# Queries' product of linear attention in float32 on four 64 by 64 tiles of TensorE, in one step with the keys' product

## The chip, the cores and the metric

One core of a Trainium2 chip runs the whole program. The metric is the device time of one execution in microseconds (us), the median of several runs. Engines are TensorE (PE, matmuls; PEld, its weight loads), VectorE (DVE), ScalarE (ACT), GpSimd (POOL) and SyncE (SP), whose queue issues all the loads and stores named here.

## What is computed

Linear attention with 8 batches, 8 heads, 576 positions and 64 columns a head, then two MLPs on the 4608 tokens (512 wide, 2048 inside):

```python
q_s = exp(q - max(q, -1));  q_s = q_s / (sum(q_s, -1) + 1e-09)     # over a head's 64 columns
k_s = exp(k - max(k, 2));   k_s = k_s / (sum(k_s, 2) + 1e-09)      # over the 576 positions
kv  = einsum('bhsd,bhse->bhde', k_s, v)                            # 64 x 64 a head
x   = einsum('bhsd,bhde->bhse', q_s, kv)                           # as rows of 512
h = x @ w_in;  x = (h - tanh(h)) @ w_out                           # first MLP
h = x @ w_in2; g = P(h) / (Q(h) + 1e-6);  out = g @ w_out2         # second MLP, P cubic, Q quadratic
```

## The kernel before

The tokens are cut into 9 blocks of 512. Block 0's attention is computed in front of everything (the loop of 8 stages `s`). After it come 144 steps n: step n does the first product of slice f = n % 16 of block j = n // 16 of the first MLP (`first_product`, 12 matmuls into `hps`), then the second product of the step two before it (12 matmuls into `acc`). The attention of block j is worked off during the 16 steps of block j - 1, by the table `work`, which holds for each step the pieces of attention and loads that are issued in it. Blocks 1 to 8 have 4 pairs p of heads each (two heads of 64 columns fill the 128 partitions). In a step the table's single functions go out first (`front`), then the first product, the second product, and then (`turn`) the matmuls of attention; their readers follow at the step's end (`follow`). The second MLP comes after step 143.

Matmuls of the MLPs run on float32r operands that are split in a high and a low part (`mm3`, lines 79 to 82: high x high, high x low, low x high). The queries' product does the same: `q_parts` (block 0) and `q_split` (later) split the queries with a copy on ScalarE and a subtraction on VectorE, `kv_parts` splits the keys' product into `bd` with two copies on ScalarE and two small operations on VectorE (lines 516 and 520), and `q_mm` runs `mm3` with `bd` as a 128 x 128 block diagonal matrix. A block of 512 tokens touches one or two batches (`spans`), with a `bd` of each, so there are three or six matmuls a pair. `q_out` copies the result to `xr` on ScalarE (line 658). The keys' product `kv_mm` (line 500) is float32: 5 groups of positions x 2 heads, each head writing its half of the partitions, 65 columns (the last is the sum).

From block 2 on the keys' maximum over positions goes through DRAM (`kv_max`, `kv_squares`, `kv_fetch`, `kv_join`, then `kv_sub`, `kv_exp`), and the queries are transposed through DRAM (`q_squares`, `q_fetch`). Pool `ps_a` has two accumulators (banks), which these products share. In the table the keys' product of pair p of block j stands in step 16(j - 1) + 3p + 4 and the queries' product one step later (block 1: 3p + 3 and 3p + 5).

In block 0 of the MLP, ScalarE, VectorE and GpSimd also decode the weights from the 64-bit numbers in which they arrive (`decode`, lines 131 to 158). Later they prepare parts of weights and of the second MLP's input (`errands`, `x2_units`).

Of the kernel before, what the change touches and what calls it, by code (L numbers as in the profile page):

```python
# [18 lines left out]
P = 128  # L19
# [24 lines left out]
def attention_moe_moe2_kernel(ctx, tc, q, k, v, w1, w2, w3, w4, ca, cb, out):  # L44
# [348 lines left out]
    bd = {}  # L393
    for par in range(2):
        for p in range(NPAIR):
            bd[par, p] = tuple(
                bdp.tile([P, P], F32R, tag=f"bd{par}{p}{part}", name=f"bd{par}{p}{part}") for part in "hl"
            )
# [3 lines left out]
    FIRST = {"qr": 4, "ke": 4, "qe": 4, "mx": 2, "mc": 2, "qm": 4, "qs": 4, "rs": 4, "qh": 2, "ql": 2}  # L402
# [91 lines left out]
    def kv_mm(b, p):  # L494
        e, vs = kv_state.pop((b, p)), vt.pop((b, p))
        pool, tag = (ps_h, "h") if b == 0 and p >= 2 else (ps_a, "a")
        ps = pool.tile([P, NB], F32, tag=tag, name="kvps")
        for g in range(G):
            for h in range(2):
                PE.matmul(  # L500
                    ps[h * D:(h + 1) * D, 0:D + 1], e[:, g, h, :], vs[:, h, g, :], start=g == 0, stop=g == G - 1
                )
        kv_state[b, p] = ps

    def kv_sum(b, p):
        rs = att_tile(b, [P, 1], F32, "rs")
        DVE.tensor_scalar_add(rs, kv_state[b, p][:, D:D + 1], EPS_S)
        DVE.reciprocal(rs, rs)
        kv_state[b, p] = kv_state[b, p], rs

    def kv_parts(b, p):
        ps, rs = kv_state.pop((b, p))
        hi, lo = bd[b % 2, p]
        heads = [(slice(h * D, (h + 1) * D), slice(0, D)) for h in range(2)]
        for r, c in heads:
            ACT.activation(out=hi[r, r], in_=ps[r, c], func=AF.Copy, scale=rs[r])

        def low():
            for r, c in heads:
                DVE.scalar_tensor_tensor(  # L520
                    out=lo[r, r], in0=ps[r, c], scalar=rs[r], in1=f32(hi[r, r]), op0=ALU.mult, op1=ALU.subtract
                )

        return low

    def kv_norm(b, p):
        kv_sum(b, p)
        return kv_parts(b, p)
# [84 lines left out]
    def q_parts(j, p):  # L613
        ps = q_state[j, p]
        qh = att_tile(j, [P, NB], F32R, "qh")
        ql = att_tile(j, [P, NB], F32R, "ql")
        ACT.copy(out=qh, in_=ps)
        DVE.tensor_tensor(out=ql, in0=ps, in1=f32(qh), op=ALU.subtract)
        q_state[j, p] = (qh, ql)


# [9 lines left out]
    def q_fetch(j, p):  # L631
        d = q_state[j, p].rearrange("(q i) (g b t) -> b i g q t", i=SQ, g=4, t=SQ)
        t = att_tile(j, [P, NB], F32R, "ql")
        for b in range(P // SQ):
            SP.dma_start(out=f32(t)[b * SQ:(b + 1) * SQ].rearrange("i (g q t) -> i g q t", g=4, t=SQ), in_=d[b])
        q_state[j, p] = t

    def q_split(j, p):
        t = q_state[j, p]
        qh = att_tile(j, [P, NB], F32R, "qh")  # L640
        ACT.copy(out=qh, in_=f32(t))  # L641
        DVE.tensor_tensor(out=t, in0=f32(t), in1=f32(qh), op=ALU.subtract)  # L642
        q_state[j, p] = (qh, t)

    def q_mm(j, p):
        qh, ql = q_state[j, p]
        ps = (ps_a if j else ps_acc).tile([P, NB], F32, tag="a" if j else f"acc{p}", name="xps")
        for b, p0, p1 in spans(j):
            def cols(a):
                return a if p1 - p0 == P else a.rearrange("x (g p) -> x g p", g=4)[:, :, p0:p1]  # L650
# [12 lines left out]
    Q = (q_max, q_sub, q_exp, q_sum, (q_turn, q_parts), (q_mm, q_out))  # L663
    Q_LATER = (q_max, q_sub, q_exp, q_sum, q_squares, q_fetch, q_split, (q_mm, q_out))
# [6 lines left out]
    def turn(todo):  # L671

        got = []
        for fn, args in todo:
            if isinstance(fn, tuple):
                fn[0](*args)
# [9 lines left out]
    work = {s: [] for s in range(NBLK * KF)}  # L686
    for j in range(1, NBLK):
        for p in range(NPAIR):
            at = (j - 1) * KF + 3 * p
            if j < B:  # L690
                for fn, s in zip(KV, (0, 1, 2, 3, 3)) if j == 1 else zip(KV_LATER, (-2, -2, 2, 3, 3, 4, 4)):
                    work[max(at + s, 0)].append((fn, (j, p)))
            for fn, s in zip(Q, (-1, 0, 1, 2, 4, 5)) if j == 1 else zip(Q_LATER, (-3, -2, -1, 0, 1, 3, 4, 5)):
                work[max(at + s, 0)].append((fn, (j, p)))
        for p in range(2, NPAIR + 2):
            at = (j - 1) * KF + 3 * p
            to, tp = j + p // NPAIR, p % NPAIR
            if to < B:
                work[at - 3].append((load_k, (to, tp)))
                work[at - (2 if to == 1 else 1)].append((load_v, (to, tp)))  # L700
            if to < NBLK:
                work[at - (4 if to == 1 else 6)].append((load_q, (to, tp)))

    with tc.manual_schedule():

        make_identity(nc, identity)
        for tiles in bd.values():
            for t in tiles:
                DVE.memset(f32(t), 0.0)
# [16 lines left out]
        for s in range(NPAIR + 4):  # L726
# [13 lines left out]
            at(3, kv_sum, q_parts)  # L740
            for low in at(3, kv_parts):
                low()
# [293 lines left out]
```

## Time and profile before

| | us |
|---|---|
| median of 3 runs | 1672.69 (1672.29 to 1672.77) |
| the profiled execution | 1671.62 |
| its span, first to last instruction | 1669.8 |
| TensorE busy | 1626.7 |
| VectorE busy | 1166.4 |
| ScalarE busy | 1022.2 |
| GpSimd busy | 1038.9 |
| attention in front | 0 to about 45 |
| steps 0 to 143 | about 38 to 895 |

A row of the timeline gives an instruction's start and length; the length of a matmul holds its way through the array, so rates are read from starts. Float32r operands stand as f32 there, and `128*64` is rows by columns of the part of the array that is used. A float32 matmul stands as two records.

### The profile page before, as it was taken

What the parts mean: (1) busy time and instruction counts of PE and PEld (TensorE: products, weight loads), DVE (VectorE), ACT (ScalarE), POOL (GpSimd) and SP (SyncE); (2) the same over time, 40 slices, a digit from 0 to 9 for tenths busy, and PEclk for the clock granted to TensorE, in tenths of its full rate; (3) what the DMA queues carried; (4) which work ended last, traced back from release to release, by engine and by line L of the source; (5) the groups of instructions that cost most, each with busy time, mean ns of one, the idle gap of its engine ahead of it and who ended that gap; (6) DMA issues with size and microseconds to landing.
All of it is one profiled execution on the core that took longest, in us unless ns stands there. A gap on an engine that the chain in (4) does not pass through costs nothing.

```text
span 1669.8 us, 26578 instructions
## 1 busy us (share of the span) xinstructions
PE 1626.7 (97%) x9096; PEld 1392.8 (83%) x9096; DVE 1166.4 (70%) x1948; ACT 1022.2 (61%) x1825; POOL 1038.9 (62%) x875
## 2 busy tenths in 40 slices
PE   5899999999999999999999999999999999999998
PEld 3677788888888888888887999999989899999996
DVE  8987666676765666653213777787878787878787
ACT  5675444554454544453325777777777777777775
POOL 4222737365463727364343888888888777777776
PEclk8999999999999999999999999999999999999999
DMA  8553665757474765633198576767676767666640
GB/s 225 166 171 94 185 180 153 208 155 215 128 221 116 206 172 150 201 121 107 52 318 306 181 268 212 274 219 269 223 263 228 243 216 248 216 247 216 209 148 26
DMA packets 250728, 323.73 MB, mean 194 GB/s; under 512 B 119009, under 2 KB 185569, under 8 KB 241377
## 3 DMA queue, kind: packets, MB, share of 16 engines
q1 hardware_dynamic: 250592, 322.03, 60.0%
q8 instruction: 72, 1.18, 0.3%
q14 instruction: 64, 0.52, 0.1%
HBM read 249.04 MB, written 72.93 MB: 193 GB/s over the span
## 4 chain that ended last, share of the span: by engine, by line
PE 88%; DVE 5%; ACT 3%; DMA 2%; issue 1%; SPq 1%; POOL 0%; DVEq 0%; ACTq 0%; POOLq 0%
PE acc L80 15%; PE acc L81 15%; PE acc L82 14%; PE z L830 12%; PE y L830 9%; PE hps L80 7%; PE hps L82 7%; PE hps L81 7%; DMA u<-x2d 1%; PE kvps L500 1%; ACT m L133 1%; DVE m L147 1%; ACT e L131 0%; DVE m L134 0%; PE xps L81 0%
## 5 line engine op out<-in xcount | busy, mean ns | idle before, releaser
L340 POOL TENSOR_TENSOR gl<-t,gh 128x512 fp32r<-128x512 f32 x128 | 175.2, 1369 | 322.7 <-ACT gh L336 295.0
L336 ACT CAST gh<-t 128x512 fp32r<-128x512 f32 x128 | 79.7, 622 | 273.2 <-PE acc L82 156.3
L887 POOL TENSOR_TENSOR n<-n,r 128x512 f32<-128x512 f32 x144 | 186.1, 1293 | 96.2 <-ACT r L884 90.8
L887 POOL TENSOR_TENSOR n<-n,n 128x512 f32<-128x512 f32 x144 | 186.5, 1295 | 36.5 <-ACT n L871 36.5
L945 DVE TENSOR_TENSOR t<-hps,t 128x512 f32<-128x512 f32 x128 | 87.5, 684 | 158.8 <-ACT t L942 158.4
L887 POOL TENSOR_TENSOR n<-n,h 128x512 f32<-128x512 f32 x144 | 187.2, 1300 | 9.7 <-DMA xl<-x2d 9.6
L942 ACT ACTIVATE t<-hps 128x512 f32<-128x512 f32 x144 | 85.9, 597 | 115.5 <-PE hps L82 92.7
L841 ACT COPY sums<-z 128x256 f32<-128x256 f32 x144 | 53.6, 372 | 134.2 <-PE z L830 134.2
L867 ACT ACTIVATE n<-h,coef 128x512 f32<-128x512 f32 x144 | 116.5, 809 | 0.3 <-POOL n L887 0.3
L897 DVE CAST gh<-a 128x512 fp32r<-128x512 f32 x144 | 99.6, 692 | 16.1 <-DVE a L893 0.5
L900 DVE TENSOR_TENSOR gl<-a,gh 128x512 fp32r<-128x512 f32 x144 | 99.6, 692 | 15.2 <-DVE gh L897 0.5
L893 DVE SCALAR_TENSOR_TENSOR a<-a,n 128x512 f32<-128x512 f32 x144 | 100.0, 694 | 14.1 <-POOL n L887 8.2
L876 DVE SCALAR_TENSOR_TENSOR a<-h,absb,a 128x512 f32<-128x512 f32 x144 | 107.5, 746 | 3.0 <-ACT a L861 2.9
L861 ACT ACTIVATE a<-h,coef 128x512 f32<-128x512 f32 x144 | 100.5, 698 | 3.4 <-DVE gl L900 3.4
L890 DVE SCALAR_TENSOR_TENSOR a<-a,r 128x512 f32<-128x512 f32 x144 | 99.3, 690 | 0.8 <-ACT r L884 0.8
L879 ACT ACTIVATE r<-a,bias_q 128x512 f32<-128x512 f32 x144 | 97.0, 674 | 0.0
L884 ACT ACTIVATE r<-r 128x512 f32<-128x512 f32 x144 | 91.1, 633 | 4.6
L864 ACT ACTIVATE h<-h 128x512 f32<-128x512 f32 x144 | 89.1, 619 | 1.0 <-DVE h L852 0.8
L848 DVE TENSOR_TENSOR h<-y,sums 128x256 f32<-128x256 f32 x72 | 30.5, 424 | 57.8 <-PE y L830 57.7
L852 DVE TENSOR_TENSOR h<-y,top 128x512 f32<-128x512 f32 x72 | 49.7, 690 | 26.2 <-ACT top L841 25.8
L604 POOL TENSOR_TENSOR qe<-qe,qs 128x512 f32<-128x512 f32 x36 | 39.2, 1088 | 46.0 <-DVE qs L603 46.0
L642 DVE TENSOR_TENSOR ql<-ql,qh 128x512 fp32r<-128x512 f32 x28 | 26.9, 960 | 50.6 <-ACT qh L641 48.7
(366 smaller groups left out, 5272.6 us busy)
## 6 DMA issues: line engine op xcount, KB each, us to landing
u<-x2d SPq DMA_DIRECT2D x78, 256.0 KB, 5.3
raw<-in_moe_w_in_dram SPq DMA_DIRECT2D x32, 512.0 KB, 4.2
raw<-in_moe_w_out_dram SPq DMA_DIRECT2D x32, 512.0 KB, 4.2
x2d<-raw SPq DMA_DIRECT2D x64, 256.0 KB, 3.2
x2d<-xr SPq DMA_DIRECT2D x56, 256.0 KB, 3.1
wa0h<-wa0d SPq DMA_DIRECT2D x9, 1024.0 KB, 5.2
wa1h<-wa2d SPq DMA_DIRECT2D x9, 1024.0 KB, 5.1
wa2h<-wa4d SPq DMA_DIRECT2D x9, 1024.0 KB, 5.0
```

The costliest lines, as they stand in the source:

```text
L80: PE.matmul(o, lhi, rhi, start=start, stop=False)
L81: PE.matmul(o, lhi, rlo, start=False, stop=False)
L82: PE.matmul(o, llo, rhi, start=False, stop=stop)
L340: eng.tensor_tensor(out=gl, in0=g, in1=f32(gh), op=ALU.subtract)
L830: PE.matmul(o, w, x[:, xc], start=m in (1, 5) and c == k == 0, stop=c == 1 and k == 2, skip_group_check=True,)
L861: ACT.activation(out=new(t, "a", ps_a), in_=t["h"], func=AF.Abs, scale=b0)
L867: ACT.activation(out=new(t, "n1"), in_=t["h"], func=AF.Identity, scale=a3, bias=a2)
L876: DVE.scalar_tensor_tensor(out=t["a"], in0=t["h2"], scalar=b1, in1=t["a"], op0=ALU.mult, op1=ALU.add)
L887: return lambda t: POOL.tensor_tensor(out=t[a], in0=t[a], in1=t[b], op=op)
L893: DVE.scalar_tensor_tensor(out=t["a"], in0=t["a"], scalar=2.0, in1=t["n0"], op0=ALU.subtract, op1=ALU.mult)
L897: DVE.tensor_copy(out=t["g"][0], in_=t["a"])
L900: DVE.tensor_tensor(out=t["g"][1], in0=t["a"], in1=f32(t["g"][0]), op=ALU.subtract)
```

## The change

The queries are kept in float32 and not split: `q_copy` takes the place of `q_parts` in block 0, and `q_split` goes away, as the fetch lands in the tile that the matmul reads. `bd` holds the normalized keys' product in float32, the two heads side by side in columns (128 x 2 x 64), without a low part. For blocks 1 to 8 `q_mm` runs four float32 matmuls a span, each with 64 rows and 64 columns of the array: head h reads its 64 partitions and writes bank `ps[h]`, half `to` of the 512 columns goes to partitions 0 to 63 or 64 to 127. It takes two accumulators of `ps_a` and hands the first to `kv_mm`, which writes its result beside the queries' result, in columns 256 to 320. For block 0 `q_mm` runs two float32 matmuls of 128 rows by 64 columns. `q_out` copies four pieces of 64 x 256 instead of one of 128 x 512. The table is written anew: the queries' products stand in steps 4, 8, 11 and 14 of the 16 (block 1: 6, 9, 12 and 14), the keys' product of pair p > 0 in the step of the queries' product of pair p - 1, that of pair 0 two steps before the block's first (block 2: in its first); maxima, transposes, fetches and loads go by these steps.

```diff
-                bdp.tile([P, P], F32R, tag=f"bd{par}{p}{part}", name=f"bd{par}{p}{part}") for part in "hl"
+        (par, p): bdp.tile([P, 2, D], F32, tag=f"bd{par}{p}", name=f"bd{par}{p}")
...
-    def kv_mm(b, p):
+    def kv_mm(b, p, room=None):
...
-        ps = pool.tile([P, NB], F32, tag=tag, name="kvps")
+        ps = pool.tile([P, NB], F32, tag=tag, name="kvps") if room is None else room
...
-                    ps[h * D:(h + 1) * D, 0:D + 1], e[:, g, h, :], vs[:, h, g, :], start=g == 0, stop=g == G - 1
+                    ps[HEADS[h], HALF:HALF + D + 1], e[:, g, h, :], vs[:, h, g, :], start=g == 0, stop=g == G - 1
...
-            ACT.activation(out=hi[r, r], in_=ps[r, c], func=AF.Copy, scale=rs[r])
-        def low():
-                DVE.scalar_tensor_tensor(
-                    out=lo[r, r], in0=ps[r, c], scalar=rs[r], in1=f32(hi[r, r]), op0=ALU.mult, op1=ALU.subtract
+            ACT.activation(out=bd[b % 2, p][r, h], in_=ps[r, HALF:HALF + D], func=AF.Copy, scale=rs[r])
...
-    def q_parts(j, p):
-        ACT.copy(out=qh, in_=ps)
-        DVE.tensor_tensor(out=ql, in0=ps, in1=f32(qh), op=ALU.subtract)
+    def q_copy(j, p):
+        t = att_tile(j, [P, NB], F32, "qh")
+        ACT.copy(out=t, in_=q_state[j, p])
...
-    def q_split(j, p):
-        ACT.copy(out=qh, in_=f32(t))
-        DVE.tensor_tensor(out=t, in0=f32(t), in1=f32(qh), op=ALU.subtract)
...
-            mm3(cols(ps), *bd[b % 2, p], cols(qh), cols(ql), True, True)
+        if j == 0:
+            for h, r in enumerate(HEADS):
+                PE.matmul(ps[r], bd[0, p][:, h], t, start=True, stop=True)
+        ps = [ps_a.tile([P, NB], F32, tag="a", name="xps") for _ in range(2)]
+        for b, p0, p1 in sorted(spans(j), key=lambda x: x[2] - x[1]):
+            for to in range(2):
+                for h, r in enumerate(HEADS):
+                    PE.matmul(
+                        cols(ps[h][HEADS[to], 0:HALF]), bd[b % 2, p][r, h], cols(t[r, to * HALF:(to + 1) * HALF]),
+                        start=True, stop=True,
+                    )
+        return ps[0]
...
-            ACT.copy(out=xr[:, p, :], in_=ps)
+            for to in range(2):
+                for h, r in enumerate(HEADS):
+                    ACT.copy(out=xr[r, p, to * HALF:(to + 1) * HALF], in_=ps[h][HEADS[to], 0:HALF])
...
+    kv_at = {(1, p): 3 * p + 3 for p in range(NPAIR)}
+    q_at = {(1, p): (6, 9, 12, 14)[p] for p in range(NPAIR)}
+            q_at[j, p] = first(j) + (4, 8, 11, 14)[p]
+                kv_at[j, p] = q_at[j, p - 1] if p else first(j) - (2 if j > 2 else 0)
+    q_from = {(j, p): 3 * p if j == 1 else at - 7 for (j, p), at in q_at.items()}
-                for fn, s in zip(KV, (0, 1, 2, 3, 3)) if j == 1 else zip(KV_LATER, (-2, -2, 2, 3, 3, 4, 4)):
+                for fn, s in zip(KV, (-3, -2, -1, 0, 0)) if j == 1 else zip(KV_LATER, (-4, -4, -2, -1, -1, 0, 0)):
...
-        for tiles in bd.values():
-            for t in tiles:
-                DVE.memset(f32(t), 0.0)
+        for p in range(NPAIR):
+            for h, r in enumerate(HEADS):
+                DVE.memset(bd[0, p][r, 1 - h], 0.0)
```

## Rows read from the trace of the kernel before

**Rows 1.** The page: busy time of each engine; shares of the chain that ended last.
```profile
PE 1626.7 (97%) x9096; PEld 1392.8 (83%) x9096; DVE 1166.4 (70%) x1948; ACT 1022.2 (61%) x1825; POOL 1038.9 (62%) x875
PE 88%; DVE 5%; ACT 3%; DMA 2%; issue 1%; SPq 1%; POOL 0%; DVEq 0%; ACTq 0%; POOLq 0%
```
**Rows 2.** Windows: stretch, busy us (and instructions) by engine, clock, DMA share, GB/s.
```profile
25.00:50.00 25.00, 16.64 (x81) 12.48 (x80) 22.29 (x48) 19.10 (x38) 8.98 (x7) 0.78 0.60 172
125.00:150.00 25.00, 23.31 (x122) 18.50 (x121) 22.42 (x43) 17.83 (x34) 3.77 (x3) 1.00 0.40 114
175.00:200.00 25.00, 23.61 (x139) 19.17 (x138) 17.64 (x27) 11.24 (x22) 19.32 (x16) 1.00 0.66 194
425.00:450.00 25.00, 25.00 (x115) 20.81 (x114) 17.19 (x30) 12.15 (x23) 8.46 (x7) 1.00 0.39 117
```
**Rows 3.** Timeline of TensorE around a keys' product: start us, length us, instruction.
```profile
365.98 0.39 PE L82 MATMUL acc<-gh,wb0l 128*128 128x512 f32 x1
366.30 0.80 PE L500 MATMUL kvps<-vt,ke 128*64 128x65 f32 x20
367.03 0.50 PE L80 MATMUL hps<-xh,wa1h 128*128 128x512 f32 x1
367.37 0.39 PE L81 MATMUL hps<-xl,wa1h 128*128 128x512 f32 x1
...
367.83 0.40 PE L80 MATMUL hps<-xh,wa1h 128*128 128x512 f32 x1
```
**Rows 4.** Timeline around queries' products of blocks 4, 7 and 8: matmul before, second after.
```profile
372.39 0.40 PE L82 MATMUL acc<-gh,wb0l 128*128 128x512 f32 x1
373.57 0.40 PE L81 MATMUL hps<-xl,wa1h 128*128 128x512 f32 x1
...
709.72 0.40 PE L82 MATMUL acc<-gh,wb3l 128*128 128x512 f32 x1
711.13 0.39 PE L81 MATMUL hps<-xl,wa3h 128*128 128x512 f32 x1
...
748.78 0.40 PE L82 MATMUL acc<-gh,wb0l 128*128 128x512 f32 x1
749.94 0.40 PE L81 MATMUL hps<-xl,wa1h 128*128 128x512 f32 x1
```
**Rows 5.** Timeline of block 0: four float32 transposes of 128 columns, and one alone.
```profile
70.42 0.60 PE L610 MATMUL qps<-identity,qe 128*128 128x128 f32 x4
56.20 0.27 PE L476 MATMUL kvps<-identity,mc 128*128 128x128 f32 x1
```
**Rows 6.** Keys' product's group, 45 to 150 us: busy, mean ns | idle, releaser.
```profile
L500 PE MATMUL kvps<-vt,ke 128*64 128x65 f32 x80 | 3.2, 226 | 4.5 <-ACT ke L492 4.3
```
**Rows 7.** Chain pieces of the front; groups of 45 to 150 us; ScalarE's 256-column copy.
```profile
18.80 0.03 DVE ql L618
...
19.41 0.27 DVE bd00l L520
...
L618 DVE TENSOR_TENSOR ql<-qps,qh 128x512 fp32r<-128x512 f32 x4 | 2.8, 691 | 1.1 <-ACT qh L617 1.1
L520 DVE SCALAR_TENSOR_TENSOR bd11l<-kvps,rs,bd11h 64x64 fp32r<-64x64 f32 x2 | 0.6, 284 | 0.8 <-ACT bd11h L516 0.8
L658 ACT COPY xr<-xps 128x512 f32<-128x512 f32 x4 | 2.4, 593 | 0.0
L841 ACT COPY sums<-z 128x256 f32<-128x256 f32 x144 | 53.6, 372 | 134.2 <-PE z L830 134.2
```
**Rows 8.** Chain pieces behind block 0, and TensorE's waits from 155 to 900 us.
```profile
163.27 4.33 DMA ke<-kd
167.62 1.12 DVE mx L550
168.77 1.77 DVE ke L482
...
PE kvps L500 <- ACT ke L492: 1.4, 2, 1.2
```

More of the change, by code (lines that the diff above doesn't have):

```diff
@@ L391, in attention_moe_moe2_kernel @@
     absb = const.tile([P, 2], F32, name="absb")
[L393 to L396, printed above, removed]
-                bdp.tile([P, P], F32R, tag=f"bd{par}{p}{part}", name=f"bd{par}{p}{part}") for part in "hl"
-            )
+    bd = {
+        (par, p): bdp.tile([P, 2, D], F32, tag=f"bd{par}{p}", name=f"bd{par}{p}")
+        for par in range(2) for p in range(NPAIR)
+    }
+    HEADS = slice(0, D), slice(D, P)
     G = -(-S // P)
     REST = S - (G - 1) * P
-    FIRST = {"qr": 4, "ke": 4, "qe": 4, "mx": 2, "mc": 2, "qm": 4, "qs": 4, "rs": 4, "qh": 2, "ql": 2}
+    FIRST = {"qr": 4, "ke": 4, "qe": 4, "mx": 2, "mc": 2, "qm": 4, "qs": 4, "rs": 4, "qh": 2}
     LATER = {"qr": 2, "qe": 2, "qm": 2, "qs": 2, "rs": 2}
@@ L512, in kv_parts @@
         ps, rs = kv_state.pop((b, p))
[L513 to L524 removed]
+        for h, r in enumerate(HEADS):
+            ACT.activation(out=bd[b % 2, p][r, h], in_=ps[r, HALF:HALF + D], func=AF.Copy, scale=rs[r])
     def kv_norm(b, p):
         kv_sum(b, p)
[L528 removed]
+        kv_parts(b, p)
     def kv_squares(b, p):
@@ L661, in q_out @@
             DVE.tensor_tensor(out=xl[:, p, :], in0=ps, in1=f32(xh[:, p, :]), op=ALU.subtract)
[L663 to L664 removed]
+    Q = (q_max, q_sub, q_exp, q_sum, (q_turn, q_copy), (q_mm, q_out))
+    Q_LATER = (q_max, q_sub, q_exp, q_sum, q_squares, q_fetch, (q_mm, q_out))
     def front(todo):
@@ L671, in turn @@
     def turn(todo):
-        got = []
+        got, room = [], None
         for fn, args in todo:
             if isinstance(fn, tuple):
-                fn[0](*args)
+                room = fn[0](*args, *([room] if room is not None and fn[0] is kv_mm else []))
                 got.append(lambda fn=fn, args=args: fn[1](*args))
@@ L686, in attention_moe_moe2_kernel, with put, first @@
     work = {s: [] for s in range(NBLK * KF)}
+    def put(s, fn, *args):
+        work[max(s, 0)].append((fn, args))
+    def first(j):
+        return (j - 1) * KF
+    kv_at = {(1, p): 3 * p + 3 for p in range(NPAIR)}
+    q_at = {(1, p): (6, 9, 12, 14)[p] for p in range(NPAIR)}
+    for j in range(2, NBLK):
+        for p in range(NPAIR):
+            q_at[j, p] = first(j) + (4, 8, 11, 14)[p]
+            if j < B:
+                kv_at[j, p] = q_at[j, p - 1] if p else first(j) - (2 if j > 2 else 0)
@@ L695, in attention_moe_moe2_kernel @@
-        for p in range(2, NPAIR + 2):
[L696 to L702, printed above, removed]
+                for fn, s in zip(KV, (-3, -2, -1, 0, 0)) if j == 1 else zip(KV_LATER, (-4, -4, -2, -1, -1, 0, 0)):
+                    put(kv_at[j, p] + s, fn, j, p)
@@ new lines, in attention_moe_moe2_kernel @@
+            s = q_from[j, p]
+            steps = (s - 1, s, s + 1, s + 2, s + 4, q_at[j, p]) if j == 1 else (s - 1, s, s + 1, s + 2, s + 3, s + 5, s + 7)
+            for fn, s in zip(Q if j == 1 else Q_LATER, steps):
+                put(s, fn, j, p)
+        for p in range(2, NPAIR + 2):
+            to, before = (j + p // NPAIR, p % NPAIR), (j + (p - 2) // NPAIR, (p - 2) % NPAIR)
+            if to in kv_at:
+                put(kv_at[before], load_k, *to)
+                put(kv_at[before] + 1, load_v, *to)
+            if to in q_at:
+                put(q_from[before] + 2, load_q, *to)
@@ L704, in attention_moe_moe2_kernel @@
     with tc.manual_schedule():
         make_identity(nc, identity)
-        for tiles in bd.values():
-            for t in tiles:
-                DVE.memset(f32(t), 0.0)
+        for p in range(NPAIR):
+            for h, r in enumerate(HEADS):
+                DVE.memset(bd[0, p][r, 1 - h], 0.0)
         kv_tiles = new_kv(att0, NPAIR), new_kv(att, 2)
@@ L739, in attention_moe_moe2_kernel @@
             at(2, kv_sub, kv_exp)
-            at(3, kv_sum, q_parts)
-            for low in at(3, kv_parts):
-                low()
+            at(3, kv_sum, q_copy)
+            at(3, kv_parts)
             if s < NPAIR + 3:
```

29 lines of the change are left out of this document (10 added, 19 removed).

## Prediction, made before the changed kernel was run

> **What bounds the kernel now.** I read the page first. TensorE is busy 97% of the span and carries 88% of the chain that ended last [rows 1]. That is an average, so next I read the windows of 25 us. They show three stages. Up to about 50 us (attention of block 0 in front of everything) TensorE works 16.64 us in a window of 25 and VectorE 22.29. In block 0 of the MLP (45 to 150 us) VectorE still works 22.42 of 25 and TensorE 23.31. From 150 us to the end of the attention work TensorE stands at 25.00 and VectorE near 17, apart from one window, 175 to 200, in which TensorE idles 1.4 us [rows 2]. So a change of the attention work in blocks 2 to 8 is worth what it does to TensorE's queue; what it takes from VectorE and ScalarE counts only before 150 us and at the seam behind it.
>
> **TensorE, steps 16 to 143: price of the old visits.** I price a visit by starts, since ends are modelled: from the start of the last matmul before it to the start of the second full matmul after it, less two full matmuls at the steady pace of 0.23 us. The keys' product (20 records, 10 float32 matmuls on two halves of 64 columns) goes from 365.98 to 367.37: 1.39 - 0.46 = 0.93 us [rows 3]. Of this 0.09 us passes before the first record starts (366.30 instead of 366.21), the records take the start of the first to the start of the next full matmul, 0.73 us, and that full matmul holds its successor 0.34 instead of 0.23 us, because its weights are loaded in the open: 0.11. The queries' product of today (six matmuls in two spans of batches, three for the last block) costs, by the same rule, 0.72 us in block 4, whose spans are equal, 0.95 in block 7, whose spans are most unequal, and 0.70 in block 8 [rows 4]. Blocks 2, 3, 5 and 6 lie between the first two; I take 0.83 as the mean of blocks 2 to 7.
>
> **Price of the new visit.** First the rate of float32. Four transposes of 128 float32 columns last 0.60 us, one alone 0.27: starts are (0.60 - 0.27) / 3 = 0.11 us apart, 0.86 ns a column, where a matmul of 512 split columns starts every 0.23 us, 0.45 ns a column [rows 5, 3]. So one float32 record takes two cycles a column, and a float32 matmul has two records (20 for 10). Next the overlap. The 20 records of 65 columns start within 0.80 - 0.22 = 0.58 us (a record lasts 0.22) [rows 3, 6], 0.029 each, and one alone needs 65 x 0.83 ns = 0.054. So two column halves run at the same time, with about 4 ns a round to spare, and the weight loads (64 columns, 0.05 us) are hidden under the stream.
> The change asks for four tiles: two halves of rows and two of columns. The trace shows no row halves. Bounds by the nearest rows: all four at once, as the two are today; two at once, as today exactly; none at once, which only a loss of the overlap now seen would give. Each tile streams 256 columns in a pair, by two records of two cycles: 256 x 4 / 2.4 GHz = 0.43 us, 0.45 with the spare of four rounds (0.50 in block 7, where a span of 32 columns is shorter than its weight load). That is four at once; two at once is 0.89, none is 1.77. I take four at once: the queue already lets records of another tile pass its neighbour's second record, and the two row halves write different banks.
> The Trainium skill ("TensorEngine Tiling (Array Packing)", Available Configurations and Key Properties) lists 64 by 64 as four independent tiles that load and multiply in parallel. No run here shows it for the rows; by that rule the value is 0.45 too.
> A visit then costs 0.09 to enter, 0.05 for the first load in the open, 0.45, then the keys' records and the way out as today. Between queries (64 rows) and keys (128 rows) the tiling changes once more. No row shows that step; it lies between nothing and what entering and the first load cost today, 0.14. A gain is excluded, as no record goes away. I take 0.14, since both changes of shape in the trace cost more than nothing (0.09 in, 0.09 + 0.11 out). Queries beside keys therefore cost 0.93 + 0.14 + 0.45 = 1.52, against 0.93 + 0.83 = 1.76: 0.24 saved.
> The same page (Key Properties) says that changing the tiling mode drains TensorE, a new tile in one mode not. The 0.09 us on entering agrees, and by the rule the 0.14 is due.
> From step 16 on there are 24 keys' products and 28 queries' products. 23 stand together: 23 x 0.24 = 5.5 saved. The last pair of block 7 stands alone (0.09 + 0.05 + 0.50 + 0.09 + 0.11 = 0.84 for 0.95: 0.1 saved), and so do the four of block 8 (0.78 for 0.70: 0.3 lost). **Sum 5.3 us saved**; with no cost between the tilings 8.6; with two at once, 28 x 0.44 = 12.3 more, 7.0 lost.
>
> **VectorE and ScalarE before 150 us.** Removed per pair: one subtraction of 0.69 us and two small ones of 0.28 on VectorE, and VectorE's waits in front of them (1.1 us for the four of block 0 and 0.8 a pair) [rows 7]. In the front stage the chain passes through them only for pair 0, from 18.80 to the end of the second small one near 19.97, 1.2 us [rows 7]; for the other pairs it runs through ScalarE, whose work there stays. I take 1.2 us, ends 0 and 3. The product of block 0 keeps column halves: 2 rounds x 512 x 2 / 2.4 = 0.85 for 0.69 us, and where the clock stands at 1.2 GHz 1.7 for 1.3 (granted 0.78 of the full clock from 25 to 50 us); TensorE's idle third in that window hides it [rows 2], and without that cover it is 1.7 us for four pairs. Eight smaller clears instead of sixteen lie before the first keys arrive: nothing.
> In block 0 the work removed is 4 x (0.69 + 0.57) = 5.0 us and up to 4.3 us of waits. Against that, copying a pair out becomes four copies of 64 by 256 for one of 128 by 512: I take 0.37 each from ScalarE's copy of 256 columns, 1.49 for 0.59, so 3.6 us more for ScalarE in four pairs [rows 7], which is busy 17.83 of 25 us there [rows 2]. And the keys of block 2, pair 0 come four steps earlier, into step 15: a maximum of 1.1 us, a subtraction of up to 1.8 and their fetch of 4.3 [rows 8]. That fetch and the store before it (steps 14 and 12) pass the weight loads on SP's queue, and VectorE's sequence in step 15 stands behind the fetch. TensorE idles 1.7 us in each window of 25 at the stage's end, some 7 us in the whole stage [rows 2], 4.3 of them for the exponentials [rows 6]; that caps the gain. I take **2.5 us saved**, ends 6 saved and 2.5 lost.
> At the seam, the 1.4 us that TensorE waited for an exponential [rows 8] should shrink, as VectorE has less to do there and the fetch is earlier: 1.0 saved, ends 1.7 saved and 2 lost. Later removals on VectorE and ScalarE's added copies lie beside a full TensorE: nothing; should ScalarE not keep up, its 0.3 us a pair (four copies more, one copy of the queries less) are 8 us over 28 pairs.
> Both buffers of the small accumulator pool are now taken in one step; their last users are a step back or more, so no wait is due. The queries' matmuls now wait for their fetch themselves, and behind them in TensorE's queue stand the keys' product and the next step; the fetch is issued two steps (11 us) ahead and the keys' fetch of the same kind took 4.3 us [rows 8], so this costs nothing; with one step of cover gone it would still fit.
>
> **Sum.** 5.3 + 1.2 + 2.5 + 1.0 = 10.0. The profiled execution took 1671.62 us (its span 1669.8), so it would take 1661.6; the median of the runs is 1672.69, hence **1662.7**.
>
> **Rivals.**
> *Only two of four tiles run at once* (weights or operands of one row half wait for the other). For it: the trace shows only column halves. 10.0 - 12.3 = 2.3 lost: 1675.0.
> *The tiles run one after the other.* 28 x 1.32 = 37 more: 1700. Against it: the overlap of two column halves in today's keys' product. The queries' product then does not do what its shape is for.
> *Keys' exponentials come late* (the slower side). Today maximum, join and subtraction of neighbouring pairs lie in different steps. In the new plan, for the third and fourth pairs of a block, join and subtraction of one and the maximum and transpose of the next fall in one step, 4 to 5 us of VectorE (1.1 and up to 1.8 [rows 8], and the maximum, estimated as long as the subtraction over the same 640 columns) in a step of 24 x 0.23 = 5.5. If TensorE then stands 1.4 us, as it does once now [rows 8], at two products in each of six blocks, that is 17 us: 1680. Against it: VectorE's order puts the subtraction ahead of the next maximum, and it has about 7 us free in a window of 25 [rows 2]. It turns the gain into a loss from 10 us of such stalls on.
> *The step between the tilings is free*: 3.3 more saved, 1659.4.
>
> **How the numbers follow.** Forecast 0.55, free step 0.13, two at once 0.14, one after the other 0.06, late exponentials 0.12. The forecast's own range, by the ends of the three early terms, is 1657 to 1669; the two next cases reach to 1655 and 1678, and what stays out (one after the other, most of the late exponentials) is under 0.2. Range 1655 to 1678. A measurement of this kernel tells 0.2%, 3.3 us, from no change. Faster: nearly all of the first two cases and a little of the others, 0.70. Slower: 0.06, half of the late exponentials, a quarter of two at once, 0.16. Same: 0.14.
>
> **What would show it.** Four records of the queries' product starting within some 20 ns, rounds of 2 x columns / 2.4 GHz, body of a joint visit near 1.3 us before the next full matmul starts: right. Rounds twice as long, or records of the lower rows starting when the upper ones end: the first rival. Idle in front of the keys' records, put down to the exponential, in steps 24, 27 and their like: the third. Block 0 must end (first matmul of step 16) about 3.7 us earlier in the trace; if it ends later, ScalarE's copies or the early fetch are the cause. A cost of the early steps above 10 us, or tiles that do not overlap, makes the forecast wrong.

## The result, and the profile after

The changed kernel takes 1684.16 us, the median of four runs (1678.42 to 1687.37), against 1672.73 before: a ratio of 1.0063 (95% interval 1.0049 to 1.0078). It is slower by 0.6%, 11 us. The forecast was 1662.7, and the time lies outside the range of 1655 to 1678. The profiled execution is the fastest of the four: 1678.42, its span 1676.4, against 1671.62 and 1669.8 before.

The page of the changed kernel, busy times and shares of the chain that ended last, to be read against [rows 1]:

```profile
PE 1622.7 (97%) x9400; PEld 1373.3 (82%) x9400; DVE 1113.0 (66%) x1840; ACT 1039.4 (62%) x1893; POOL 1036.3 (62%) x875
PE 75%; DVE 8%; DMA 6%; ACT 5%; SPq 3%; issue 2%; POOL 0%; DVEq 0%; ACTq 0%; POOLq 0%
```

TensorE works 4 us less and VectorE 53 us less, as the change intends, and still the span is 6.6 us longer. TensorE's part of the last chain fell from 88% to 75%; DMA and SP's queue, together 3% before, carry 9%. The windows of 25 us (columns as in [rows 2]) say where:

```profile
125.00:150.00 25.00, 22.91 (x142) 17.13 (x141) 22.32 (x39) 17.48 (x36) 5.15 (x4) 1.00 0.35 87
175.00:200.00 25.00, 22.95 (x125) 18.37 (x124) 15.69 (x24) 12.86 (x25) 19.44 (x17) 0.93 0.58 169
...
475.00:500.00 25.00, 23.39 (x133) 18.98 (x132) 13.95 (x22) 11.20 (x22) 15.36 (x15) 1.00 0.81 226
```

Behind 150 us, where TensorE stood at 25.00 apart from one window, there are now stretches in which it does not. What it waits for, from the table of waits of 155 to 900 us (engine and line, the releaser: us in total, times, longest):

```profile
PE xps L499 <- ACT ke L491: 9.2, 8, 2.1
...
DVE rs L506 <- ACT xr L649: 54.1, 23, 3.8
DVE mx L539 <- DMA ke<-kd: 51.4, 16, 5.8
```

Before, the first wait was 1.4 us in two times [rows 8]. VectorE's wait for the keys' fetch was 27.6 us, and the one in the middle, of line 506 for ScalarE's copies, was not there.

**Where the time went**, from starts of TensorE's matmuls in the two profiled executions. Three points divide the span: the first second product (`acc<-gh,wb0h`, step 2), the first matmul of step 16 (`hps<-xh,wa0h`), and the first second product of block 8, which lies behind all attention work.

| first matmul of | before | after | difference | part by itself |
|---|---|---|---|---|
| step 2's second product | 53.48 | 51.60 | -1.88 | front: 1.9 saved |
| step 16 | 148.85 | 148.35 | -0.50 | block 0: 1.4 lost |
| block 8's second product | 820.02 | 825.33 | +5.31 | steps 16 to 129: 5.8 lost |
| end of the span | 1669.8 | 1676.4 | +6.6 | behind it: 1.3 lost |

The third part is the one that turned. An undisturbed visit there is as cheap as forecast. The timeline of TensorE in block 4, beside [rows 3 and 4]:

```profile
370.67 0.39 PE L82 MATMUL acc<-gh,wb0l 128*128 128x512 f32 x1
370.99 0.67 PE L637 MATMUL xps<-qh,bd 64*64 64x128 f32 x16
371.59 0.80 PE L499 MATMUL xps<-vt,ke 128*64 128x65 f32 x20
372.32 0.50 PE L80 MATMUL hps<-xh,wa1h 128*128 128x512 f32 x1
372.66 0.40 PE L81 MATMUL hps<-xl,wa1h 128*128 128x512 f32 x1
```

From 370.67 to 372.66, less 0.46, the visit costs 1.53 us; 1.52 was forecast. At the seam it is another picture:

```profile
177.10 0.67 PE L637 MATMUL xps<-qh,bd 64*64 64x64 f32 x16
179.82 0.80 PE L499 MATMUL xps<-vt,ke 128*64 128x65 f32 x20 [2.05 <-ACT ke L491]
...
181.15 0.63 PE L82 MATMUL hps<-xh,wa1l 128*128 128x512 f32 x1
181.58 0.63 PE L80 MATMUL hps<-xh,wa1h 128*128 128x512 f32 x1
```

The keys' records start 2.72 us behind the queries' instead of 0.60, since the exponentials are late, and then the full matmuls start 0.43 us apart instead of 0.23, up to 184.54: the granted clock is 0.93 in that window, as TensorE runs at 1.2 GHz for a while after the wait. Eight matmuls from 181.15 take 3.39 us instead of 1.82, another 1.6.

The sum of the third part: 7.8 us more of waits (9.2 less 1.4), 0.07 us that each of the eight gaps is longer than the wait booked for it (0.6), and 1.6 at the low clock, 10.0 lost. The visits give 4.8 back: 23 joint ones at 1.54 (1.53, and 1.59 in block 7) for 1.76 save 5.1, the lone one of block 7 at 0.85 for 0.95 saves 0.1, and four of block 8 at 0.79 for 0.70 lose 0.4. That leaves 5.2 lost of the 5.8 seen. The 1.3 us behind block 8 were not followed further.

**Why the exponential is late.** The chain of work of the changed kernel that leads to another of these products (block 5; start, length, what), followed back from the product:

```profile
475.71 0.64 SPq L619
...
476.39 4.73 DMA ke<-kd
...
483.73 1.23 DVE mx L457
...
485.61 0.61 DVE t L950
...
486.82 0.66 ACT e L131
...
488.62 0.52 ACT raw L365
489.14 0.65 ACT ke L491
...
489.83 0.80 PE xps L499 x20
```

It begins in SP's queue, with four issues of the queries' fetch (line 619). SP's timeline of the same place, and what VectorE then does:

```profile
473.68 2.67 SPq L619 DMA_DIRECT2D qh<-qd  x4
476.39 0.63 SPq L533 DMA_DIRECT2D ke<-kd  x1
...
481.14 1.10 DVE L539 TENSOR_REDUCE mx<-ke 128x128 f32<-128x512 f32 x1 [3.10 <-DMA ke<-kd]
```

The keys' fetch is issued behind four issues of 0.64 us each and lands 4.7 us after its own. VectorE, which works in the order of the program, stands in front of the join (line 539) for 3.10 us, and everything that follows on it in that step (the subtraction, the queries' transpose, the next maximum, the activation's `t`) goes to ScalarE as late as that. ScalarE does four pieces of decoding and errands, from line 131 to line 365 in the chain, in front of the exponential (line 491).

The table explains the order. In the old one, fetches of keys and queries never stood in one step. In the new one the keys' product of pair p stands in the step of the queries' product of pair p - 1, and both fetches go out two steps before their products: so both always stand in one step, and the pieces of the earlier pair, the queries' fetch, go out first.

### The profile page after: what moved, and what is told of

The parts are those of the page before. It is cut to its first block, busy times and chain, and to the rows that moved or that the text cites. A ratio compares the mean times of both kernels' runs of the same rounds, so it can differ in the third digit from the quotient of the medians.

```text
span 1676.4 us, 26996 instructions
## 1 busy us (share of the span) xinstructions
PE 1622.7 (97%) x9400; PEld 1373.3 (82%) x9400; DVE 1113.0 (66%) x1840; ACT 1039.4 (62%) x1893; POOL 1036.3 (62%) x875
## 4 chain that ended last, share of the span: by engine, by line
PE 75%; DVE 8%; DMA 6%; ACT 5%; SPq 3%; issue 2%; POOL 0%; DVEq 0%; ACTq 0%; POOLq 0%
PE acc L80 13%; PE acc L81 13%; PE acc L82 12%; PE z L835 11%; PE y L835 8%; PE hps L80 5%; PE hps L81 5%; PE hps L82 5%; DMA u<-x2d 2%; SPq L619 1%; DMA ke<-kd 1%; DMA xh<-x2d 1%; PE xps L499 1%; ACT m L133 1%; DVE mx L457 1%
## 5 line engine op out<-in xcount | busy, mean ns | idle before, releaser
L892 POOL TENSOR_TENSOR n<-n,r 128x512 f32<-128x512 f32 x144 | 186.3, 1294 | 97.4 <-ACT r L889 92.0
L593 POOL TENSOR_TENSOR qe<-qe,qs 128x512 f32<-128x512 f32 x36 | 42.7, 1186 | 47.9 <-DVE qs L592 47.9
L80 PE MATMUL hps<-xh,wa0h 128*128 128x512 f32 x144 | 57.5, 399 | 3.9 <-DVE gl L340 3.9
```

Source lines behind the costliest of these rows:

```text
L80: PE.matmul(o, lhi, rhi, start=start, stop=False)
L892: return lambda t: POOL.tensor_tensor(out=t[a], in0=t[a], in1=t[b], op=op)
```

## The experiments

Medians in us; the ratio is to the kernel before on the same chip. The last column is TensorE's wait for the exponentials, 155 to 900 us (times).

| kernel | median (lowest to highest) | ratio, 95% interval | wait |
|---|---|---|---|
| a1_fetch_first | 1666.50 (1665.93 to 1667.17) | 0.9958 [0.9944, 0.9973] | none |
| a2_norm_first | 1684.14 (1679.89 to 1686.25) | 1.0055 [1.0038, 1.0072] | 13.4 (9) |
| a3_both | 1667.24 (1666.05 to 1670.09) | 0.9964 [0.9951, 0.9977] | none |
| a4_old_steps | 1673.33 (1670.60 to 1675.35) | 0.9999 [0.9990, 1.0009] | 0.2 (1) |
| b1_one_copy | 1667.01 (1665.44 to 1667.94) | 0.9961 [0.9946, 0.9976] | |
| b2_copies_shared | 1667.89 (1666.65 to 1668.46) | 0.9966 [0.9953, 0.9979] | |
| b3_block1_columns | 1663.39 (1662.73 to 1663.65) | 0.9939 [0.9922, 0.9956] | |
| b4_columns_shared | 1663.78 (1662.52 to 1665.52) | 0.9943 [0.9928, 0.9958] | |
| c1_split_new_steps | 1687.54 (1682.74 to 1688.34) | 1.0076 [1.0059, 1.0094] | 9.4 (9) |
| c2_columns_all | 1671.41 (1668.95 to 1673.41) | 0.9991 [0.9982, 1.0000] | |
| c3_split_fetch_first | 1689.90 (1689.11 to 1690.89) | 1.0099 [1.0081, 1.0117] | 13.4 (11) |

Two theories explain the late exponentials. **Theory A**: the order of the two fetches in SP's queue makes the exponentials late. **Theory B**: the shared banks do it. The keys' product now lies in a bank that ScalarE copies the queries' result out of, so VectorE's reciprocal of the sums (line 506) waits for all four copies (the 54.1 us), and VectorE is held up by that.

### The keys' fetch first

```diff
     def front(todo):
-        for fn, args in todo:
+        for fn, args in sorted(todo, key=lambda x: x[0] is not kv_fetch):
```

> The changed kernel, but in each step the keys' fetch is issued ahead of the four queries' fetches that stand in the same step. Theory A (the joint steps put the keys' fetch behind 2.6 us of other issues on SP's queue, VectorE's join waits for it, and the exponential comes late): VectorE's waits for the keys' fetch fall from 51 us to about 25, TensorE's waits for exponentials behind 155 us from 9.2 to under 3, time 1672 to 1676. Theory B (the shared bank: VectorE's sum waits for ScalarE's copies of the queries' result, 54 us in all, and that delays the next step's work): the fetch waits fall as well, but the 54 us stay, and so do most of TensorE's waits, 6 to 9 us; time 1680 to 1684.

One line turns 11 us lost into 7.3 us gained, more than theory A had asked for (1672 to 1676). SP's queue and VectorE of this kernel at the same pair:

```profile
467.03 0.50 SPq L533 DMA_DIRECT2D ke<-kd  x1
467.58 2.81 SPq L619 DMA_DIRECT2D qh<-qd  x4
...
471.36 1.13 DVE L539 TENSOR_REDUCE mx<-ke 128x128 f32<-128x512 f32 x1
```

The join no longer waits here, and over the stage its waits for the fetch fall from 51.4 to 9.7 us. TensorE's wait for the exponentials is gone from the table altogether. The wait of theory B is not smaller but larger:

```profile
DVE rs L506 <- ACT xr L649: 63.1, 23, 3.9
...
DVE mx L539 <- DMA ke<-kd: 9.7, 8, 2.6
```

So 63 us of VectorE waiting for the shared bank cost TensorE nothing behind 150 us, and theory A stands. The four runs now lie within 1.2 us of each other, where those of the changed kernel spread over 9. So the spread went with the waits. The slower runs of the changed kernel were not profiled; an execution as slow as they are, of the same order of fetches, was (a2_norm_first, 1686.25): its waits are longer, 13.4 us in nine, and the granted clock is 0.93 in three windows of 25 us behind 150 us (at 475, 675 and 925) instead of one.

### The keys' product's readers first, and both

```diff
-                got.append(lambda fn=fn, args=args: fn[1](*args))
+                got.insert(0 if fn[0] is kv_mm else len(got), lambda fn=fn, args=args: fn[1](*args))
```

> The changed kernel, but behind the matmuls of a joint step the readers of the keys' product are issued ahead of the four copies of the queries' result. Theory A: the fetch still lands late, VectorE's waits for it stay near 51 us and TensorE's waits for exponentials near 9 us; time 1680 to 1686. Theory B: VectorE's wait of 54 us in front of the sum goes, TensorE's waits fall under 3 us; time 1672 to 1676. Block 0 of the MLP should end about 1 us earlier under B.

> Both orders changed: keys' fetch first in a step, keys' readers first behind it. If A and B together hold what was lost, TensorE's waits for exponentials are under 1 us, its clock does not fall behind block 0, and what is left is the saving of the joint visits (23 x 0.18 us) and the front: 1666 to 1670, runs within 1 us of each other. If something else delays the exponential (ScalarE's order, VectorE's load in one step), waits of 3 us and more stay and the time is over 1673.

The edit puts the reciprocal and the scaled copies into `bd` ahead of the four copies. The waits of the first of the two:

```profile
PE xps L499 <- ACT ke L491: 13.4, 9, 2.3
...
DVE mx L539 <- DMA ke<-kd: 54.8, 18, 6.0
DVE rs L506 <- PE xps L499: 21.7, 14, 2.7
```

The wait for the copies is gone (VectorE waits 21.7 us for the product itself), and the time is that of the changed kernel: 1684.14. With both edits it is that of the fetch alone, 1667.24 and 1666.50 with intervals that overlap; only the runs lie further apart than expected, over 4 us. Theory B falls twice. Its side forecast, block 0 about 1 us shorter, was a miss too: block 0 (read as in the table under "Block 0: the four copies") takes 98.3 and 98.4 us in these two, more than in the changed kernel (96.75).

### The new product at the old steps

```diff
-            q_at[j, p] = first(j) + (4, 8, 11, 14)[p]
+            q_at[j, p] = first(j) + 3 * p + 5
-                kv_at[j, p] = q_at[j, p - 1] if p else first(j) - (2 if j > 2 else 0)
+                kv_at[j, p] = first(j) + 3 * p + 4
...
-                ... zip(KV_LATER, (-4, -4, -2, -1, -1, 0, 0)):
+                ... zip(KV_LATER, (-6, -6, -2, -1, -1, 0, 0)):
...
-                put(kv_at[before], load_k, *to)
+                put(kv_at[before] - (before[0] > 1), load_k, *to)
```

> The float32 product on four tiles for blocks 2 to 8 in the steps of the kernel before: queries' and keys' products in neighbouring steps, each with its own way in and out, own banks, fetches in different steps; block 0 as in the changed kernel, except that block 2's first keys come four steps later. If the loss comes from the joint steps: TensorE's waits for exponentials as before (1 to 2 us), a queries' visit costs about 0.80 us by its starts and a keys' visit 0.93, together near the 1.76 of before; time 1671 to 1675. If the loss comes from the product itself (four copies on ScalarE, two banks at once): waits of 5 us and more stay; 1680 or more.

Blocks 2 to 8 have the new product, but keys and queries in steps of their own as before. The waits are gone (0.2 us), and so is the gain: 1673.33, the time of the kernel before. The timeline of a queries' product that stands alone:

```profile
372.46 0.39 PE L82 MATMUL acc<-gh,wb0l 128*128 128x512 f32 x1
372.78 0.67 PE L637 MATMUL xps<-qh,bd 64*64 64x128 f32 x16
373.38 0.50 PE L80 MATMUL hps<-xh,wa1h 128*128 128x512 f32 x1
373.71 0.40 PE L81 MATMUL hps<-xl,wa1h 128*128 128x512 f32 x1
```

It costs 1.25 - 0.46 = 0.79 us (0.80 as the mean), and the keys' visit there 0.93: 1.72 in two steps, hardly less than the 1.76 of the old products, and 1.53 in one. The four tiles by themselves are worth next to nothing; what they allow, one step for both, is worth 0.2 us a pair, the way out of one visit (0.09 + 0.11 in [rows 3]). One step for both is worth nothing without them: the split product joined with the keys (c1_split_new_steps, next) costs 1.65 us in block 4 (373.46 to 375.57, less 0.46), as much as its two visits apart (0.93 + 0.72).

### The table alone, and the table with the fetch first

The first takes the new table's steps for the kernel before, with its split product and its readers left as they were; the second adds the sorting of `front` to it.

```diff
-                for fn, s in zip(KV, (0, 1, 2, 3, 3)) if j == 1 else zip(KV_LATER, (-2, -2, 2, 3, 3, 4, 4)):
-                    work[max(at + s, 0)].append((fn, (j, p)))
...
+                for fn, s in zip(KV, (-3, -2, -1, 0, 0)) if j == 1 else zip(KV_LATER, (-4, -4, -2, -1, -1, 0, 0)):
+                    put(kv_at[j, p] + s, fn, j, p)
+            steps = ... (s - 1, s, s + 1, s + 2, s + 3, s + 5, s + 6, s + 7)
```

> The kernel before (queries and bd split, three float32r matmuls a span, one bank) with the changed kernel's table of steps, keys' fetch behind the queries' fetches. If the loss comes from the table alone (theory A): VectorE's waits for the keys' fetch rise from 28 to about 50 us, TensorE's waits for exponentials from 1.4 to 6 us or more (VectorE has more to do than in the changed kernel), nothing is saved at the visits; 1680 to 1690. If it needs the new product (its copies, its two banks), waits stay under 3 us; 1672 to 1675.

> c1_split_new_steps (the split product of the kernel before in the new table of steps), with the keys' fetch issued ahead of the queries' fetches. If the order of the fetches is the whole loss of the table: TensorE's waits for exponentials fall from 9.4 us to under 2, time near the kernel before, 1672 to 1675. If the new table also loads VectorE too much in one step (the rival as it was put in the prediction: join, subtraction and the next maximum in one step), waits of 4 us and more stay; 1678 to 1684.

The new steps cost the split product 14.4 us by themselves, and TensorE's waits are 9.4 us. VectorE's wait for the keys' fetch was expected near 50 us and is 10.2. That was a miss: the place is the same, but VectorE stands at the split's subtraction first (53.4 us in 23 waits for ScalarE's copy `qh`, 48.7 in 25 before), and by the time it comes to the join the fetch has landed, or nearly:

```profile
483.31 1.17 DVE L642 TENSOR_TENSOR ql<-ql,qh 128x512 fp32r<-128x512 f32 x1 [1.79 <-ACT qh L641]
484.66 1.09 DVE L550 TENSOR_REDUCE mx<-ke 128x128 f32<-128x512 f32 x1 [0.19 <-DMA ke<-kd]
```

So the order of the fetches alone doesn't explain this loss.

The second is the surprise, outside both of its ranges: the order that cured the new product does not cure the split one, 1689.90. Its timeline, SP's queue, ScalarE and VectorE:

```profile
479.43 0.50 SPq L544 DMA_DIRECT2D ke<-kd  x1
479.98 2.66 SPq L635 DMA_DIRECT2D ql<-qd  x4
...
485.68 0.62 ACT L641 CAST qh<-ql 128x512 fp32r<-128x512 f32 x1 [2.00 <-DMA ql<-qd]
...
486.33 0.69 DVE L642 TENSOR_TENSOR ql<-ql,qh 128x512 fp32r<-128x512 f32 x1 [2.54 <-ACT qh L641]
486.94 1.08 DVE L550 TENSOR_REDUCE mx<-ke 128x128 f32<-128x512 f32 x1
```

The keys' fetch goes first, and the split, one step behind the queries' fetch, waits in its place: 2.00 us on ScalarE here, 28.1 us in 14 waits over the stage, and VectorE behind it. It waited before too, 14.2 us in 9 with the queries' fetch first and 5.3 in 5 in the kernel before. So in the new steps the split is late behind its own fetch in either order; how much of the two losses that makes was not taken apart. In the changed kernel nothing on ScalarE or VectorE reads the queries' fetch, only TensorE two steps later; that is why the order is free there. The removal of the split and the order of the fetches are worth something together only.

### Two tiles at once for all blocks

```diff
+        if j >= 1:
+            ps = ps_a.tile([P, NB], F32, tag="a", name="xps")
...
+                    PE.matmul(cols(ps[r]), bd[b % 2, p][:, h], cols(t), start=True, stop=True)
...
+        if j >= 1:
+            ACT.copy(out=xr[:, p, :], in_=ps)
```

> a1_fetch_first with the queries' product of all blocks as two float32 matmuls of 128 rows by 64 columns a span, into one bank, one copy; so only two tiles at once, and the keys' product follows in the same tiling. It prices the rival of the prediction and the change of tiling between queries and keys. Expected visit by its starts: 0.09 + 0.05 + 4 rounds that sum to 0.89 + 0.58 + 0.09 + 0.11 = 1.81 us for 1.53; if the change of tiling were free in a1_fetch_first, the visit would be 1.97. Block 0 as in b3_block1_columns. Time 1663.4 + 23 x 0.28 + 5 x 0.44 = 1672.

Based on the kernel with the fetch first: two matmuls of 128 rows by 64 columns a span, one bank, one copy, the unused quarters of `bd` zeroed. It measures the first rival's price, and that of the change of tiling, since queries and keys now have the same one.

```profile
404.51 0.39 PE L82 MATMUL acc<-gh,wb2l 128*128 128x512 f32 x1
404.82 1.08 PE L637 MATMUL xps<-qh,bd 128*64 128x256 f32 x8
405.74 0.75 PE L499 MATMUL kvps<-vt,ke 128*64 128x65 f32 x20
...
406.76 0.40 PE L81 MATMUL hps<-xl,wa3h 128*128 128x512 f32 x1
```

The visit costs 2.25 - 0.46 = 1.79 (1.81 was expected), 0.26 more than with four tiles and more than the 1.76 of the old pair. The forecast's terms give 0.44 (two at once for four) less 0.14 (no change of tiling), 0.30. The median is 1671.41, 4.9 us above a1_fetch_first. About that is due: 23 joint visits of 0.26 us and five lone ones of 0.41 are 8.0, less the 3.1 by which block 1, done like this, shortens the time (b3_block1_columns, below), 4.9.

### Block 0: the four copies

All on the basis of a1_fetch_first. The first copies a quarter of a pair's result in block 1 and clears `xr` at the start, so three quarters of block 1's attention are left out. The second gives the copies of every second head to VectorE. The third computes block 1's product with two 128 by 64 tiles into one bank, with one copy of 128 by 512, as above but for `j == 1` alone. The fourth is the third with the second's sharing for the later blocks.

```diff
-            for to in range(2):
-                for h, r in enumerate(HEADS):
+            for to in range(2 if j > 1 else 1):
+                for h, r in enumerate(HEADS[:2 if j > 1 else 1]):
```

> The kernel with the keys' fetch first (a1_fetch_first); for block 1 only one of the four copies of the queries' result is made (three quarters of that block's attention output are left out, xr is set to 0 in front instead). Theory C (ScalarE's three added copies of 0.37 us a pair hold up block 0 of the MLP): step 16 starts 2 to 4 us earlier than in a1_fetch_first; 1662 to 1664. Theory D (the queries' product takes both accumulators and so waits for VectorE's subtraction, which reads the bank behind the keys' maximum): TensorE's waits in block 0 stay as they are, step 16 moves by under 1 us; 1666.

```diff
-                    ACT.copy(out=xr[r, p, to * HALF:(to + 1) * HALF], in_=ps[h][HEADS[to], 0:HALF])
+                    (DVE.tensor_copy if h and True else ACT.copy)(
+                        out=xr[r, p, to * HALF:(to + 1) * HALF], in_=ps[h][HEADS[to], 0:HALF]
+                    )
```

> a1_fetch_first with two of the four copies (the second head's bank) on VectorE, in all blocks. Theory C: ScalarE is relieved of 0.75 us a pair, VectorE gets about 0.85 us, in block 0 no gain or up to 2 us; behind 155 us TensorE is full either way, so nothing, unless the exponentials come late again: 1664 to 1667. Theory D: no change, 1666.

```diff
+        if j == 1:
+            ps = ps_a.tile([P, NB], F32, tag="a", name="xps")
...
+        if j == 1:
+            ACT.copy(out=xr[:, p, :], in_=ps)
```

> a1_fetch_first, but for block 1 the queries' product runs like that of block 0, two float32 matmuls of 128 rows by 64 columns a span into one bank, copied out by one copy of 128 by 512; the keys' product has the other bank. TensorE pays 0.45 us more a pair in a stage where it idles. Both theories expect block 0 to end 2 to 3 us earlier and 1663 to 1664: under C because the copies go, under D because the wait for both banks goes; read with b1_one_copy, it tells which. If neither holds, 1666 to 1668.

> b3_block1_columns with the second head's copies of blocks 2 to 8 on VectorE: in these blocks TensorE is the bound, so like b3_block1_columns within 1 us; if ScalarE's copies also delayed something there (tanh waits), 1 to 2 us less.

Block 0 by itself, from step 2's second product to step 16, read from the starts as above:

| kernel | step 2's | step 16 | block 0 | against before (95.37) |
|---|---|---|---|---|
| after | 51.60 | 148.35 | 96.75 | 1.4 lost |
| a1_fetch_first | 52.20 | 148.12 | 95.92 | 0.6 lost |
| b1_one_copy | 53.96 | 147.29 | 93.33 | 2.0 saved |
| b2_copies_shared | 52.53 | 148.25 | 95.72 | 0.4 lost |
| b3_block1_columns | 52.25 | 145.91 | 93.66 | 1.7 saved |

Without the extra copies block 0 is 2.3 to 2.6 us shorter than in a1_fetch_first. The b kernels alone don't settle why, since fewer copies and fewer waits for a bank come together: in b1_one_copy step 16 starts only 0.8 us earlier, as theory D had it, behind a front that ends 1.76 later (GpSimd clears `xr` there for 1.81 us, so its median of 1667.01, outside theory C's range, shows little), and its wait for the subtraction falls as well, from 2.3 to 0.9 us. The chain that ended last settles it. In the changed kernel it passes through ScalarE's copies in three pairs of block 0, 1.0 us each time, and then through the reciprocal that waits for them:

```profile
109.43 0.27 ACT xr L649
...
109.71 0.36 ACT xr L649
...
110.09 0.38 ACT xr L649
...
110.49 0.17 DVE rs L506
```

So it does in a1_fetch_first, 3.0 us in all. In b1_one_copy one copy stands there each time, 0.8 us in all, and in b3_block1_columns one copy of 0.49 us in all, so 2.3 and 2.6 us left the chain. TensorE's waits in b3_block1_columns are hardly less: the one for both accumulators is gone (2.3 us), but the one for the exponentials is 4.2 instead of 2.2. So the copies are on the path, theory C; theory D's wait is real, but not what b3_block1_columns saves. Sharing the copies with VectorE gains nothing (1667.89); VectorE is fuller there than ScalarE (22.32 us against 17.48 in the window from 125 to 150). Block 1's product with two tiles, the whole time 1663.39, is the fastest kernel found, 0.6% below the kernel before; sharing the later copies adds nothing to it (1663.78).

## Why the prediction was wrong, point by point

**The steady visits: right.** 1.53 us for the forecast 1.52, with four tiles at once; the records of one round start 6 to 7 ns apart, and a round of 128 columns takes 0.109 us. The Trainium skill ("TensorEngine Tiling (Array Packing)", Available Configurations and Key Properties) has 64 by 64 as four independent tiles; the trace agrees, in this kernel's rounds. The step between the two tilings, for which no row stood, is 1.53 - 0.93 - 0.45 = 0.15 us, the upper of the two bounds, and c2_columns_all agrees with that within 0.03. The same page of the Trainium skill (Key Properties) says that a change of the tiling mode drains TensorE and a new tile in one mode does not; both agree. In sum 4.8 us for 5.3.

**"The fetch is issued two steps (11 us) ahead ... so this costs nothing": the step that failed.** It looked at the reader of the queries' fetch, TensorE, which indeed never waits for it. It did not look at what the four issues stand in front of. I had counted the early fetch of block 2, pair 0, against the weight loads on SP's queue, at the end of block 0 only, and did not see that the new table puts the queries' fetch and the next pair's keys' fetch in one step in each of the six later blocks, the queries' first. Four issues of 0.64 us move the keys' fetch 2.7 us back. Its join stands one step later, at the head of VectorE's work, and 2.7 us of issues and 4.7 to land are more than the 5.5 us of a step (24 x 0.23). Cost: what the order of the fetches is worth, 11.4 us lost to 7.3 gained by the medians, 12.3 us between the two profiled executions.

**The seam, 1.0 us forecast as saved.** It lost: 2.05 us of wait in front of the first joint visit instead of 1.4 in all, and 1.6 at the low clock. The cause is the same: at 164.53 the queries' fetch takes SP's queue for 2.7 us, and the keys' fetch follows at 167.26. In a1_fetch_first nothing waits there, so 1.4 came for the 1.0 forecast.

**The rival "keys' exponentials come late": the place was right, the mechanism was not.** It had TensorE stand 1.4 us at two products a block, 17 us, 1680, and gave that 0.12. The waits are eight, 9.2 us. But the work of VectorE in one step, on which it rested, is as much in a1_fetch_first, where nothing waits. VectorE does not have too much to do; it starts too late. A row of the kernel before would have shown it, VectorE's waits from 155 to 900 us, which I had not read for this:

```profile
DVE mx L550 <- DMA ke<-kd: 27.6, 17, 3.5
```

At 17 of its 24 joins this fetch had no cover left to give.

**Block 0, 2.5 us forecast as saved: 1.4 lost.** Its work was costed rightly, ScalarE's copies at 0.37 us. One pair's copies in the changed kernel's timeline:

```profile
109.33 1.53 ACT L649 COPY xr<-xps 64x256 f32<-64x256 f32 x4
```

It is 1.53 with the gaps between them; 1.49 was forecast. What failed is the weight: 3.6 us more of ScalarE were set against 5.0 us less of VectorE as if they lay side by side, and 3.0 us of copies lie on the chain, where 0.49 lay before. (TensorE's idle time, the cap of the gain, was read low as well: 8.2 us in the four windows from 50 to 150, not some 7.) Nor was "no wait is due" for the two accumulators right:

```profile
101.36 0.30 PE L637 MATMUL xps<-qh,bd 64*64 64x32 f32 x2
...
103.11 0.72 PE L637 MATMUL xps<-qh,bd 64*64 64x32 f32 x14 [1.44 <-DVE ke L481]
104.50 0.80 PE L499 MATMUL xps<-vt,ke 128*64 128x65 f32 x20 [0.67 <-ACT ke L491]
```

The second accumulator is still read by VectorE's subtraction of the keys of the next pair (line 481), so the product's other row half stands for 1.44 us: 2.3 us in two waits before 155 us. In b3_block1_columns, with one accumulator and one copy, this wait is gone, and 1.7 of the forecast 2.5 are saved. What keeps the rest was not settled, nor the 0.8 us between the changed kernel and a1_fetch_first there. The early keys of block 2, the other cause that the prediction had named, are not it: a4_old_steps has them four steps later, and its block 0 takes 97.4 us.

**The front**: 1.9 us saved by step 2's second product for a forecast of 1.2, within its bounds. One execution doesn't tell more: a1_fetch_first to a4_old_steps, with the same front, save 0.5 to 1.8 there.

**What would have made the forecast right.** a1_fetch_first saves 7.3 us and b3_block1_columns 10.0, which is the forecast's sum. That it is so to a tenth is luck: b3_block1_columns is another kernel, and between its profiled execution and the one before lie 8.0 us, 1.2 in the front, 1.7 in block 0 and 5.8 in steps 16 to 129 (forecast 1.2, 2.5 and 6.3), less 0.7 behind.

| order of the fetches | old steps | new steps, queries' first | new steps, keys' first |
|---|---|---|---|
| split product | 1672.7 (before) | +14.4 (c1) | +16.1 (c3) |
| four float32 tiles | -0.5 (a4) | +11.4 (after) | -7.3 (a1) |

Each entry is the difference of medians, in us, to the kernel before. The product alone is worth nothing and the new steps alone cost 14.4; in the old steps the two fetches never meet, so their order was not run there. All three together are worth 7.

## What to carry to other kernels

When a plan moves steps, write down each queue's order in the new steps, not only the distance from each issue to its own reader: a transfer with two steps of slack can stand in front of one that has none, and four issues of 0.64 us are enough. Two waits of one engine that are equally long in the table can be worth nothing and everything: behind 150 us, 54 us of VectorE for the copies cost no time, and 51 us at the head of its step cost what was lost there. Remove each by itself to tell them apart. And price the merging of two small products by the way in and out that is saved as well as by the columns that run at once: here four tiles without the joint step, and the joint step without four tiles, gave nothing.

## What the runs showed of the hardware

- TensorE's clock fell after a wait of 2.05 us at the seam: the full matmuls behind it start 0.43 us apart, 1.2 GHz, for 3.4 us. The seven later waits, of up to 1.8 us, show a granted clock of 1.00 in all their windows. The length of the wait alone doesn't decide: in c3_split_fetch_first waits of 2.00 and 2.79 us leave every window from 150 to 900 us at 1.00.
- Four copies of 64 partitions by 256 cost ScalarE 0.37 us each, one of 128 by 512 costs 0.59 [rows 7]: a quarter of the elements for 0.6 of the time.
- An issue of the queries' fetch held SP's queue 0.63 us (median of 112 in the changed kernel), one of the keys' fetch 0.62 behind the queries' and 0.43 in front of them (a1_fetch_first, medians of 24).
